# Decode step with cached attention and a bilinear GLU on one core: first five loads in three, last head's V weighed in two places

## The chip, the core and the metric

One core of a Trainium2 chip. The metric is the device time of one execution in microseconds (us), as the median over runs. The core has a matrix engine (TensorE, "PE" in the profile, its weight loads "PEld"), a vector engine (VectorE, "DVE"), a scalar engine (ScalarE, "ACT"), a general engine (GpSimd, "POOL"), and a sync engine (SyncE, "SP") that here issues all transfers. 16 DMA engines move data from the chip's memory (HBM) into the on-chip memory (SBUF), which has 128 partitions. TensorE writes its results into PSUM.

## The reference

One decode step for two sequences (B = 2): layernorm of x, attention of 32 heads over the last 2048 positions of a K and V cache, a bilinear GLU, and a residual. All in float32.

```python
B, Sq, D = 2, 1, 512
Hq, Hkv, Sk, Dh = 32, 32, 8192, 128          # F = 1376
W = min(4096, max(256, Sk // 4))             # 2048
xn = _layernorm(x)
q = (xn @ wq).reshape(B, Sq, Hq, Dh)...
scores = einsum("bhqd,bhkd->bhqk", q, k[:, :, Sk - W:]) * Dh ** -0.5
o = einsum("bhqk,bhkd->bhqd", softmax(scores), v[:, :, Sk - W:])
out = x + o.reshape(B, Sq, Hq * Dh) @ wo + ((xn @ w_gate) * (xn @ w_up)) @ w_down
```

The caches that are read make 2 x 2 x 32 x 2048 x 128 x 4 bytes = 134 MB; with the weights the core reads 159.5 MB, each byte once, for little arithmetic.

## The kernel before

**Layout of the data.** The host lays all inputs out as one long array, `stream`, in the order in which the kernel wants them. `blocks()` (L40) lists it: each block belongs to a tile (the key) and has fields, of which each is so many columns of 128 partitions. `("k", h)` is the K of head h for both sequences (4096 columns, 2 MB), `("v", h)` its V, `("wq", h)` a part of the query projection for a later group of heads, `("wo", h)` head h's rows of the output projection (512 columns), `("w", 0)` and `("w", 1)` the query projection of the first group (first head, other three), `("wg"/"wu", half)` halves of the gate and up projections, `("wd", i)` 128 rows of w_down. `wd(n)` takes the rows `WD[n]`. One block is one DMA.

**Buffers and queue.** There are three big SBUF tiles (`BUFS = 3`) of 13,824 columns. `pump()` (L137) issues on SP's queue the loads for which a tile is free; `done()` (L163) counts a field as used up, and with a tile's last field the tile is free and `pump()` goes on. So a load waits for the last reader of the tile three loads earlier. Only the first block, with key `q` (x, w part 0, three tables of ones called pick, rows and carry, and x once more as rows, `xr`, for the residual), has a small tile of its own, `first`. Loads 1 to 4 after it bring head 0's K with w part 1; the first half of gate and up with head 1's K; the second half with head 2's K; head 3's K, head 0's V and five blocks of w_down. Then follow 18 loads of three units each (a unit is the K of one head or the V of one, which runs `LAG = 3` heads behind K). The end: head 31's K with head 28's V; then into one tile head 29's V and head 30's V, one load each; into the last tile head 31's V in two halves (`v0`, and `v1` with wo), w_down's blocks 5 to 7, 8 and 9, and its last 96 rows, which come from a second array.

**Per head.** DVE multiplies K by the broadcast q in place (`products`, L265) and sums over 128 elements (`sums`, L273), 4.42 us each. `maxima` and `weights` (L278, L286) make the softmax numerators with DVE, POOL and ACT; `reciprocals` their sums. `weigh` (L317) multiplies V by them on TensorE, 4 matmuls per sequence and head into one of two PSUM tiles `o_ps`; `copy_out` (L326) brings these to SBUF on ACT and changes to the other tile; `transpose` (L333) is 4 small matmuls with `pick` and an ACT copy that scales by the reciprocals; `project_o` (L352) multiplies by wo. In the trace each TensorE operation in float32 shows as two matmuls.

**The output sum.** Up to head `HF - 1 = 25`, results add up in `acc`, 17 rows by 512. For the tail the sum changes its form: `accumulate` (L305) writes four matmuls of 128 columns, each to its own rows, so that the last addition and the output need only 128 columns. The old sum is carried over by a copy to SBUF (`acc_sb`, on DVE) and a matmul with `carry`. `down` (L409) adds the w_down blocks: part 0 to `acc`, the later ones by `accumulate`.

**Order.** Each engine runs its instructions in the order in which they are written (`InOrder`, L77). `keep_busy(n)` is a matmul of n columns whose result nobody reads. The tail, from L449, is written out by hand: head 30's and 31's K on DVE; on TensorE heads 26 and 27, then 28, 29, 30 and 31, each weighing, transposes, projection, with fillers between. At the end stand w_down's parts 1 and 2, head 31's projection, and the residual (`o_out`, L486), then the output's DMA.

Of the kernel before, what the change touches and what calls it, by code (L numbers as in the profile page):

```python
# [35 lines left out]
STEP = 3 * UNIT  # L36
WD = [(0, 5), (5, 8), (8, NFC)]


def blocks():  # L40

    def wd(n):
        return [("wd", i, D) for i in range(*WD[n])]

    def k(h):
        first = [("w", 1, CQ - NC * DH)] if h == 0 else []
        return [("k", h, CK)] + first + ([("wq", h, CP)] if h + HG < H else [])

    def v(h):
        return [("v", h, CK), ("wo", h, CO)]

    def gu(half):
        n = NC * (FH[half][1] - FH[half][0])
        return [("wg", half, n), ("wu", half, n)]  # L60

    units = []
    for h in range(LAG, H - 1):
        units += [k(h), v(h - LAG)]
    loads = [k(0), gu(0) + k(1), gu(1) + k(2), units[0] + units[1] + wd(0)]
    loads += [sum(units[i : i + 3], []) for i in range(2, len(units), 3)]
    loads += [k(H - 1) + v(H - 1 - LAG)]
    ones = [("pick", 0, 8 * B), ("rows", 0, NFB * B), ("carry", 0, M)]
    out = [(("q", 0), [("x", 0, B * NC), ("w", 0, NC * DH)] + ones + [("xr", 0, P)])]
    out += [(("s", i), fields) for i, fields in enumerate(loads)]  # L70
    late, last = ("s", len(loads)), ("s", len(loads) + 1)
    out += [(late, v(H - 3)), (late, v(H - 2)), (last, [("v0", H - 1, CK // 2)])]
    out += [(last, [("v1", H - 1, CK // 2), ("wo", H - 1, CO)])]
    return out + [(last, wd(n)) for n in range(1, len(WD))]

# [32 lines left out]
def kernel(  # L108
    ctx: ExitStack,
    tc: tile.TileContext,  # L110
    stream: bass.AP,
    wd_rest: bass.AP,
# [24 lines left out]
    def pump():  # L137
        nonlocal held
        while todo:
            key, fields, at = todo[0]  # L140
            if key not in tiles:
                if key[0] == "q":
                    n = sum(w for _, _, w in fields)
                    tiles[key] = const.tile([P, n], F32, name="first")
                elif held == BUFS:
                    return
                else:
                    held += 1
                    tiles[key] = steps.tile([P, STEP], F32, name="step")
# [12 lines left out]

    def done(kind, i):  # L163
        nonlocal held
        _, key = got.pop((kind, i))
        left[key] -= 1
        if left[key] == 0 and key[0] != "q":
# [6 lines left out]
    pick = got["pick", 0][0].rearrange("p (r s b) -> p r s b", s=2, b=B)  # L174
    rows, carry, x_nat = got["rows", 0][0], got["carry", 0][0][:M], got["xr", 0][0]

# [21 lines left out]
    for t in oT_ring:  # L198
# [10 lines left out]
        xc, xT, tr[:, 0:B].unsqueeze(2).to_broadcast([P, B, NC]), op=ALU.subtract  # L209
    )  # L210
    dve.tensor_tensor(sq, xc, xc, op=ALU.mult)
    dve.tensor_reduce(st[:, 1, :], sq, axis=AX.X, op=ALU.add)
# [10 lines left out]
        xnb, xn.rearrange("p c b -> p (c b)").unsqueeze(2).to_broadcast([P, NC * B, P])  # L223
    )

    q_ps, s_t, mm_t, p_t, sum_t, rec_t, o_sbs, oT = {}, {}, {}, {}, {}, {}, {}, {}
# [23 lines left out]
    def project_q(h):  # L250

        g, c = h // HG + 1, h % HG
        if c == 0:
# [98 lines left out]
    def project_o(h):  # L352
        wo = got["wo", h][0]
        if h < HF:
            pe.matmul(acc, oT.pop(h), wo, start=(h == 0), stop=(h == HF - 1))
        else:
            accumulate(oT.pop(h), wo)
        done("wo", h)
# [50 lines left out]
    def down(n):  # L409
        for c in range(*WD[n]):  # L410
            if n == 0:
                pe.matmul(acc, hT[:, c % 4, c // 4, :], got["wd", c][0], start=False, stop=False)
            else:
                accumulate(hT[:, c % 4, c // 4, :], got["wd", c][0])
            done("wd", c)


    HF = H - 6
    spare_in = xnb.rearrange("p a b -> p (a b)")
    project_first(0)  # L420
    for _, fields in blocks()[1:]:
        ks = [i for kind, i, _ in fields if kind == "k"]
        vs = [i for kind, i, _ in fields if kind == "v"]
        if not ks:
            break
        if vs and vs[-1] >= H - 5:
            break
        for n, h in enumerate(ks):
            products(h)
            if h == 0:  # L430
                project_first(1)
            if h + HG < H:
                project_q(h)
# [25 lines left out]
    keep_busy(GC)  # L459
    accumulate(carry, acc_sb)  # L460
    project_o(HF)
    project_o(HF + 1)
    keep_busy(GC)
# [3 lines left out]
    sums(h + 1)  # L467
    values([H - 4], ((GC, 256), (GC,)))
    weights(h)
# [22 lines left out]
def laid_out(x):  # L492

    import numpy as np

    a = x["A_x"].reshape(B, D)
    first = {
        kind: np.zeros((P, w), a.dtype) for kind, _, w in blocks()[0][1] if kind != "w"
    }
    first["x"][:] = a.reshape(B, P, NC).transpose(1, 0, 2).reshape(P, B * NC)  # L500
    for b in range(B):
# [5 lines left out]
        first["carry"][RB * b, RB * b] = 1.0  # L507
        first["xr"][RB * b :: 32, :] = a[b].reshape(D // P, P)
    cache = {
# [31 lines left out]
    ]  # L541
    return {"stream": np.concatenate(parts), "wd_rest": wd[NFC * P :]}

# [30 lines left out]
```

## Time and profile before

| | |
|---|---|
| median of 3 runs | 379.82 us (379.79 to 380.61) |
| the profiled execution: time | 380.0 us |
| its span, first to last instruction | 378.2 us |
| HBM read | 159.54 MB, 422 GB/s over the span |
| DVE busy | 294.2 us (78%) |
| PE busy | 258.9 us (68%) |
| ACT busy | 58.2 us (15%) |
| mean granted TensorE clock | 0.788 |

The page of the profile cuts the span in 40 slices, with a digit for the busy share of each engine in tenths. The chain of waits is followed back from the last instruction: at each step to what released it. In a timeline a line has the start, the time, engine, line of the kernel (nearly all have L92, the helper that keeps the order), operation, tiles out<-in, count, and the idle time before it with what ended it. A window's line has busy times and counts of PE, PEld, DVE, ACT and POOL, then the granted clock, the busy share of the DMA engines and their rate.

### The profile page before, as it was taken

To read this page: it belongs to the slowest core of one execution; us is meant where nothing else is said; L and a number is where in the kernel's file an instruction comes from. 1 tells how busy PE (TensorE), PEld (TensorE's weight loads), DVE (VectorE), ACT (ScalarE), POOL (GpSimd) and SP (SyncE) were. 2 spreads that over 40 slices of the span, in tenths; PEclk is the share of its full clock that TensorE was granted. 3 is DMA by queue.
4 is the path that set the end of the run, shared out by engine and by line. 5 is a ranking of instruction groups with operands and counts; after the bars stand their busy time and mean duration, and the time that the engine had idled before them with its cause. 6 is when DMAs were issued, how large, how long until landed. Compare 5 with 4: busy or idle time off the path is not lost.

```text
span 378.2 us, 2866 instructions
## 1 busy us (share of the span) xinstructions
PE 258.9 (68%) x1090; PEld 88.4 (23%) x1090; DVE 294.2 (78%) x144; ACT 58.2 (15%) x255; POOL 25.4 (7%) x78
## 2 busy tenths in 40 slices
PE   3929878848557487854838685485867638637986
PEld 3501222312122122211212221121212203022433
DVE  3739762999499499859949976994997799599950
ACT  1020012102020211202021120111102011111231
POOL 1000000001000000000000010000000000000000
PEclk9967968868596966859686688976669888556999
DMA  8999999999999999999999999999999999999993
GB/s 328 475 411 421 465 444 404 462 427 415 459 393 456 450 404 450 429 415 462 398 451 446 404 450 433 421 452 428 415 456 409 440 446 433 434 411 425 414 415 141
DMA packets 4456, 159.71 MB, mean 422 GB/s; under 512 B 500, under 2 KB 508, under 8 KB 988
## 3 DMA queue, kind: packets, MB, share of 16 engines
q1 hardware_dynamic: 4444, 159.54, 98.0%
q8 instruction: 8, 0.13, 0.1%
q14 instruction: 4, 0.03, 0.0%
HBM read 159.54 MB, written 0.00 MB: 422 GB/s over the span
## 4 chain that ended last, share of the span: by engine, by line
DMA 67%; PE 16%; DVE 14%; ACT 1%; issue 0%; SPq 0%; DVEq 0%
DMA step<-in_stream_dram 67%; PE o_ps L92 8%; DVE s L92 7%; DVE step L92 7%; PE q L92 5%; PE acc L92 2%; PE tr L92 1%; ACT o_sb L92 1%; ACT oT L92 0%; SPq L92 0%; DVE m L92 0%; DVE o_out L92 0%; DVE rec L92 0%; DVEq L92 0%
## 5 line engine op out<-in xcount | busy, mean ns | idle before, releaser
L92 DVE TENSOR_TENSOR step<-step,q 128x4096 f32<-128x4096 f32 x31 | 136.6, 4407 | 59.8 <-DMA step<-in_stream_dram 59.8
L92 PE MATMUL q<-step,xnb 128*128 128x512 f32 (+1 forms) x128 | 94.8, 888 | 75.5 <-DMA step<-in_stream_dram 75.5
L92 DVE TENSOR_REDUCE s<-step 128x32 f32<-128x4096 f32 x32 | 141.4, 4420 | 1.1
L92 PE MATMUL o_ps<-step,p 128*16 128x512 f32 x512 | 70.7, 688 | 10.4 <-DMA step<-in_stream_dram 10.4
L92 PEld LDWEIGHTS q<-step,xnb 128*128 128x128 f32 x128 | 32.4, 278 | 130.2 <-DMA step<-in_stream_dram 78.4
L92 PE MATMUL acc<-step,oT 128*17 128x512 f32 (+1 forms) x100 | 34.8, 518 | 9.8 <-ACT oT L92 9.8
L92 ACT COPY o_sb<-o_ps 128x512 f32<-128x512 f32 x24 | 14.0, 585 | 148.1 <-PE o_ps L92 148.1
L92 PE MATMUL tr<-first,o_sb 128*128 128x2 f32 (+2 forms) x192 | 26.2, 257 | 14.5 <-ACT o_sb L92 12.8
L92 PEld LDWEIGHTS tr<-first,o_sb 128*128 128x128 f32 x192 | 24.6, 197 | 34.9 <-ACT o_sb L92 32.2
L283 POOL PARTITION_ALL_REDUCE mm<-m x32 | 11.3, 354 | 299.3 <-DVE rec L92 191.0
L92 PEld LDWEIGHTS o_ps<-step,p 128*16 128x16 f32 x512 | 13.4, 107 | 73.9 <-issue 58.8
L92 ACT ACTIVATE nm<-mm 128x2 f32<-128x2 f32 x32 | 6.5, 203 | 129.4 <-POOL mm L283 129.4
L92 ACT ACTIVATE p<-s,nm 128x16 f32<-128x16 f32 x64 | 19.2, 300 | 1.0
L92 ACT ACTIVATE oT<-tr,rec 128x1 f32<-128x1 f32 x64 | 12.2, 260 | 28.3 <-PE tr L92 28.3
L299 POOL PARTITION_ALL_REDUCE sum<-rs x32 | 12.7, 398 | 41.0 <-ACT p L92 41.0
L92 PE MATMUL o_ps<-step,xn 128*2 128x512 f32 (+1 forms) x48 | 13.0, 597 | 0.0
L92 ACT ACTIVATION_READ_ACCUMULATOR p<-s,nm 128x1 f32 x64 | 12.0, 187 | 0.0
L92 PE MATMUL q<-xnb,mean_w 128*128 128x512 f32 (+1 forms) x24 | 11.6, 580 | 0.0
L92 PEld LDWEIGHTS acc<-step,oT 128*17 128x17 f32 x100 | 4.8, 98 | 18.6 <-ACT oT L92 12.5
L92 DVE TENSOR_TENSOR step<-step,tr 128x4096 f32<-128x4096 f32 x1 | 4.4, 4420 | 3.9 <-DMA step<-in_stream_dram 3.9
L92 PE MATMUL acc<-step,hT 128*17 128x128 f32 (+2 forms) x58 | 7.3, 350 | 0.0
L92 DVE TENSOR_TENSOR o_out<-acc,first 128x128 f32<-128x128 f32 x1 | 0.3, 290 | 8.9 <-PE acc L92 8.9
(34 smaller groups left out, 39.7 us busy)
## 6 DMA issues: line engine op xcount, KB each, us to landing
step<-in_stream_dram SPq DMA_DIRECT2D x16, 6912.0 KB, 31.1
step<-in_stream_dram SPq DMA_DIRECT2D x2, 6400.0 KB, 30.0
step<-in_stream_dram SPq DMA_DIRECT2D x1, 6656.0 KB, 29.2
step<-in_stream_dram SPq DMA_DIRECT2D x1, 5888.0 KB, 30.0
step<-in_stream_dram SPq DMA_DIRECT2D x2, 2304.0 KB, 16.0
step<-in_stream_dram SPq DMA_DIRECT2D x1, 4352.0 KB
step<-in_stream_dram SPq DMA_DIRECT2D x1, 3712.0 KB, 33.1
step<-in_stream_dram SPq DMA_DIRECT2D x1, 3072.0 KB, 10.1
```

What stands on the lines that cost most here:

```text
L92: made = call(*args, **kwargs)
L283: nc.gpsimd.partition_all_reduce(mm, m, P, bass_isa.ReduceOp.max)
L299: nc.gpsimd.partition_all_reduce(sum_t[h], rs, P, bass_isa.ReduceOp.add)
```

## The change

- **First loads.** The block `q` and its tile `first` are gone. x, the three tables, both parts of w and the K of heads 0 and 1 (with their wq parts) are one load of 11,311 columns into a big tile. The second load has the first half of gate and up with head 2's K (12,800 columns), the third the second half with head 3's K, head 0's V and three blocks of w_down (13,568). These three fill the three tiles. The tables are copied to a small tile `ones` by three DVE copies, as their big tile is to be freed.
- **Residual.** x as rows comes by a DMA of its own from a small array, 8 rows of 512 bytes, into a tile that DVE has set to zero. It stands fourth on SP's queue.
- **Start of the computation.** Both parts of the first projection run one after the other before head 0's products. The GLU halves go with heads 2 and 3 rather than 1 and 2, and `gate()` stands in head 3's turn ahead of head 0's values.
- **w_down.** Parts (0,3), (3,5), (5,8), (8,10): blocks 3 and 4 move from load 4 to the load of head 31's K. They are added to `acc` by `down(1)` after head 28's weighing. `HF` is 28 rather than 26, so heads 26 and 27 go to `acc` too, and the copy `acc_sb` is made later, on ACT.
- **Last loads.** Head 31's second half of V is a load of its own; its wo comes with w_down's blocks 5 to 7.
- **Tail.** Head 31's first half is weighed after head 30's weighing and one filler, ahead of head 30's transposes, where ACT copies head 30's result. Of the fillers there, one of 512 and the one of 512 between the two halves become two of 256.

```diff
-WD = [(0, 5), (5, 8), (8, NFC)]
+WD = [(0, 3), (3, 5), (5, 8), (8, NFC)]
...
-        first = [("w", 1, CQ - NC * DH)] if h == 0 else []
-        return [("k", h, CK)] + first + ([("wq", h, CP)] if h + HG < H else [])
+        return [("k", h, CK)] + ([("wq", h, CP)] if h + HG < H else [])
...
-    loads = [k(0), gu(0) + k(1), gu(1) + k(2), units[0] + units[1] + wd(0)]
+    ones = [("pick", 0, 8 * B), ("rows", 0, NFB * B), ("carry", 0, M)]
+    first = [("x", 0, B * NC)] + ones + [("w", 0, NC * DH), ("w", 1, CQ - NC * DH)]
+    loads = [first + k(0) + k(1), gu(0) + k(2), gu(1) + units[0] + units[1] + wd(0)]
     loads += [sum(units[i : i + 3], []) for i in range(2, len(units), 3)]
-    loads += [k(H - 1) + v(H - 1 - LAG)]
-    ones = [("pick", 0, 8 * B), ("rows", 0, NFB * B), ("carry", 0, M)]
-    out = [(("q", 0), [("x", 0, B * NC), ("w", 0, NC * DH)] + ones + [("xr", 0, P)])]
-    out += [(("s", i), fields) for i, fields in enumerate(loads)]
+    loads += [k(H - 1) + v(H - 1 - LAG) + wd(1)]
+    out = [(("s", i), fields) for i, fields in enumerate(loads)]
...
-    out += [(last, [("v1", H - 1, CK // 2), ("wo", H - 1, CO)])]
-    return out + [(last, wd(n)) for n in range(1, len(WD))]
+    out += [(last, [("v1", H - 1, CK // 2)]), (last, [("wo", H - 1, CO)] + wd(2))]
+    return out + [(last, wd(n)) for n in range(3, len(WD))]
...
+    x_nat = const.tile([P, P], F32, name="x_nat")
+    dve.memset(x_nat, 0.0)
+    sp.dma_start(x_nat[::RB, :], x_rows)
...
+    for kind in ("pick", "rows", "carry"):
+        t = got[kind, 0][0]
+        n += t.shape[1]
+        dve.tensor_copy(ones[:, n - t.shape[1] : n], t)
+        done(kind, 0)
...
-            if n == 0:
-                pe.matmul(acc, hT[:, c % 4, c // 4, :], got["wd", c][0], start=False, stop=False)
+            if n < 2:
+                pe.matmul(
+                    acc, hT[:, c % 4, c // 4, :], got["wd", c][0],
+                    start=False, stop=(c == WD[1][1] - 1),
+                )
...
-    HF = H - 6
+    HF = H - 4
...
-            if 1 <= h <= 2:
-                project_gu(h - 1)
+            if 2 <= h <= 3:
+                project_gu(h - 2)
             sums(h)
+            if h == LAG:
+                gate()
             if vs and n == 0:
                 values(vs)
             if h == LAG:
                 down(0)
-            if h == 2:
-                gate()
...
-    acc_sb = const.tile([M, D], F32, name="acc_sb")
-    dve.tensor_copy(acc_sb, acc)
     products(h)
     sums(h)
-    o_sb = pv([HF, HF + 1])
-    keep_busy(GC)
-    keep_busy(256)
-    transpose([HF, HF + 1], o_sb)
-    keep_busy(GC)
-    accumulate(carry, acc_sb)
-    project_o(HF)
-    project_o(HF + 1)
+    values([H - 6, H - 5], ((GC, 256), (GC,)))
     keep_busy(GC)
...
-    values([H - 4], ((GC, 256), (GC,)))
+    o_sb = pv([HF])
+    down(1)
+    acc_sb = const.tile([M, D], F32, name="acc_sb")
+    act.copy(acc_sb, acc)
+    transpose([HF], o_sb)
+    keep_busy(256)
+    accumulate(carry, acc_sb)
+    project_o(HF)
...
-    values([H - 2], ((GC,), ()))
+    o_sb = pv([H - 2])
+    keep_busy(256)
     weigh(H - 1, 0, got["v0", H - 1][0], True, False)
-    keep_busy(GC)
+    transpose([H - 2], o_sb)
+    keep_busy(256)
+    project_o(H - 2)
     weigh(H - 1, 1, got["v1", H - 1][0], False, True)
     o_sb = copy_out()
     keep_busy(256)
     transpose([H - 1], o_sb)
-    down(1)
+    down(2)
     project_o(H - 1)
-    down(2)
+    down(3)
```

More of the change, by code (lines that the diff above doesn't have):

```diff
@@ L110 @@
     tc: tile.TileContext,
+    x_rows: bass.AP,
     stream: bass.AP,
@@ L141, in pump @@
             if key not in tiles:
[L142 to L145, printed above, removed]
+                if held == BUFS:
                     return
-                else:
-                    held += 1
-                    tiles[key] = steps.tile([P, STEP], F32, name="step")
+                held += 1
+                tiles[key] = steps.tile([P, STEP], F32, name="step")
                 used[key] = 0
@@ L166, in done @@
         left[key] -= 1
-        if left[key] == 0 and key[0] != "q":
+        if left[key] == 0:
             del tiles[key]
@@ L173 @@
     xT = got["x", 0][0].rearrange("p (b c) -> p b c", b=B)
-    pick = got["pick", 0][0].rearrange("p (r s b) -> p r s b", s=2, b=B)
-    rows, carry, x_nat = got["rows", 0][0], got["carry", 0][0][:M], got["xr", 0][0]
+    x_nat = const.tile([P, P], F32, name="x_nat")
+    dve.memset(x_nat, 0.0)
+    sp.dma_start(x_nat[::RB, :], x_rows)
     mean_w = const.tile([P, P], F32, name="mean_w")
@@ L210 @@
     )
+    done("x", 0)
     dve.tensor_tensor(sq, xc, xc, op=ALU.mult)
@@ L224 @@
     )
+    ones = const.tile([P, sum(w for _, _, w in blocks()[0][1][1:4])], F32, name="ones")
+    n = 0
+    for kind in ("pick", "rows", "carry"):
[3 more added lines that the diff above has]
+        done(kind, 0)
+    pick = ones[:, : 8 * B].rearrange("p (r s b) -> p r s b", s=2, b=B)
+    rows, carry = ones[:, 8 * B : 8 * B + NFB * B], ones[:M, 8 * B + NFB * B :]
     q_ps, s_t, mm_t, p_t, sum_t, rec_t, o_sbs, oT = {}, {}, {}, {}, {}, {}, {}, {}
@@ L250, in project_q @@
     def project_q(h):
+        if h + HG >= H:
+            return
         g, c = h // HG + 1, h % HG
@@ L354, in project_o @@
         if h < HF:
-            pe.matmul(acc, oT.pop(h), wo, start=(h == 0), stop=(h == HF - 1))
+            pe.matmul(acc, oT.pop(h), wo, start=(h == 0), stop=False)
         else:
@@ L415, in down @@
             done("wd", c)
-    HF = H - 6
+    HF = H - 4
     spare_in = xnb.rearrange("p a b -> p (a b)")
-    project_first(0)
-    for _, fields in blocks()[1:]:
+    for i in range(2):
+        project_first(i)
+    for _, fields in blocks():
         ks = [i for kind, i, _ in fields if kind == "k"]
         vs = [i for kind, i, _ in fields if kind == "v"]
-        if not ks:
-            break
         if vs and vs[-1] >= H - 5:
@@ L429 @@
             products(h)
[L430 to L433, printed above, removed]
[L434 to L435 removed]
+            project_q(h)
+            if 2 <= h <= 3:
+                project_gu(h - 2)
             sums(h)
+            if h == LAG:
+                gate()
             if vs and n == 0:
@@ L497, in laid_out @@
     first = {
-        kind: np.zeros((P, w), a.dtype) for kind, _, w in blocks()[0][1] if kind != "w"
+        kind: np.zeros((P, w), a.dtype) for kind, _, w in blocks()[0][1][:4]
     }
@@ L507, in laid_out @@
         first["carry"][RB * b, RB * b] = 1.0
-        first["xr"][RB * b :: 32, :] = a[b].reshape(D // P, P)
     cache = {
@@ L541, in laid_out @@
     ]
-    return {"stream": np.concatenate(parts), "wd_rest": wd[NFC * P :]}
+    return {
+        "x_rows": a.reshape(B, D // P, P).transpose(1, 0, 2).reshape(-1, P),
+        "stream": np.concatenate(parts), "wd_rest": wd[NFC * P :],
+    }
 _INS = ["A_x", "A_k_cache", "A_v_cache", "A_wq", "A_wo", "B_w_gate", "B_w_up", "B_w_down"]
```

## The prediction

> **What bounds the kernel now.** First the head of the page and its chain of waits.
>
> ```profile
> span 378.2 us, 2866 instructions
> DMA  8999999999999999999999999999999999999993
> DMA 67%; PE 16%; DVE 14%; ACT 1%; issue 0%; SPq 0%; DVEq 0%
> ```
>
> The DMA engines are busy in every slice but the first and the last, and two thirds of the chain is waiting for a landing. Busy shares of the other engines (DVE 78%, PE 68%) hide that. Next, the windows, to see where the stream begins and ends (columns: window, length, busy time and count of PE, PEld, DVE, ACT, POOL, granted clock, DMA share, GB/s).
>
> ```profile
> 1.00:2.00 1.00, 0.00 (x0) 0.00 (x0) 0.85 (x2) 1.00 (x1) 0.81 (x9) 1.00 0.42 55
> 2.00:3.00 1.00, 0.00 (x0) 0.00 (x0) 0.60 (x2) 0.00 (x1) 0.00 (x0) 1.00 0.96 327
> 3.00:4.00 1.00, 0.03 (x1) 0.03 (x1) 0.16 (x1) 0.00 (x0) 0.00 (x0) 1.00 0.99 364
> 1.70:371.50 369.80, 255.22 (x1024) 85.70 (x1024) 293.15 (x140) 56.21 (x252) 24.19 (x67) 0.78 1.00 431
> 371.50:373.20 1.70, 1.62 (x12) 0.93 (x8) 0.00 (x0) 0.58 (x1) 0.00 (x0) 1.00 0.51 189
> ```
>
> From 1.7 to 371.5 us the share is 1.00 at 431 GB/s: there is no hole in the stream, so a shorter compute stage in the middle is worth nothing. Only three things can move the end: the bytes, the slow first microseconds, and what is left to do after the last loads land. For that last part, the issues of the final loads with their time to landing, and the TensorE timeline of the tail.
>
> ```profile
> step<-in_stream_dram SPq DMA_DIRECT2D x1, 1280.0 KB, 14.5
> step<-in_stream_dram SPq DMA_DIRECT2D x1, 1024.0 KB, 11.8
> step<-in_stream_dram SPq DMA_DIRECT2D x1, 768.0 KB, 16.1
> step<-in_stream_dram SPq DMA_DIRECT2D x1, 512.0 KB, 16.9
> step<-in_wd_rest_dram SPq DMA_DIRECT2D x1, 192.0 KB, 16.9
> ```
>
> ```profile
> 364.30 1.91 PE L92 MATMUL o_ps<-step,p 128*16 128x512 f32 x16 [0.44 <-DMA step<-in_stream_dram]
> 366.13 1.13 PE L92 MATMUL q<-xnb,mean_w 128*128 128x512 f32 x2
> 367.10 0.95 PE L92 MATMUL tr<-first,o_sb 128*128 128x2 f32 x8
> 368.55 0.41 PE L92 MATMUL acc<-step,oT 128*17 128x128 f32 x8 [0.50 <-ACT oT L92]
> 368.78 1.04 PE L92 MATMUL o_ps<-step,p 128*16 128x512 f32 x8
> 369.75 1.13 PE L92 MATMUL q<-xnb,mean_w 128*128 128x512 f32 x2
> 370.81 1.05 PE L92 MATMUL o_ps<-step,p 128*16 128x512 f32 x8
> 371.79 0.70 PE L92 MATMUL q<-xnb,mean_w 128*128 128x256 f32 x2
> 372.56 1.05 PE L92 MATMUL tr<-first,o_sb 128*128 128x2 f32 x8
> 373.55 0.85 PE L92 MATMUL acc<-step,hT 128*17 128x128 f32 x24
> ```
>
> SP's timeline has those loads issued at 355.32, 354.94, 355.79, 356.26 and 356.73 us (in the order of the rows), so they land at 369.8 (second half of head 31's V), 366.7 (first half), 371.9, 373.2 and 373.6. Head 30's V landed at 364.25 (the chain's DMA piece ends there). From then TensorE is the bound: it has no idle time but 0.50 us, and o_out starts at 375.34, 1.7 us after the last landing. The `q<-xnb,mean_w` rows are fillers that compute nothing.
>
> **The change, part by part.** The sum is made against the profiled execution: span 378.2, time 380.0, so 1.8 us lies around the span. The median of the runs is 379.82; I take the difference off that.
>
> *Tail (−1.3).* After v30's matmuls the order becomes: filler of 256, first half of head 31, transposes of head 30, filler of 256, projection of head 30, second half of head 31, then as before. In start-to-start times of the rows above: head 30's weighing 1.83 (366.13−364.30); filler of 256, half of the 512's 1.06 (370.81−369.75), 0.53; half a head 0.97 (369.75−368.78); transposes and the way to the projection 1.45 (368.55−367.10), of which the second filler covers the ACT wait, so 0.96+0.53 = 1.49; projection 0.23; from the second half to o_out 4.53 (375.34−370.81). Sum 9.58, against 11.04 (375.34−364.30) now: −1.46. Two landings answer back. The first half, landing 2.5 us after v30, is wanted 2.36 us after: +0.1. The second half now lands alone, 256 KB less at 431 GB/s, so at 369.2, before it is wanted at 369.45. wo with three w_down blocks ends at the byte where w_down's first part ended (371.9) and is wanted at 372.2. The last landing, 373.63, stays where it is, and behind it stand the last 8 matmuls, about 0.4 (24 of them plus the drain took 375.34−374.33 = 1.01): o_out not before 374.08. So the tail gives 375.34−374.08 = 1.26.
>
> *Head 28's stage (0, covered).* down(1), two 512-wide projections (2×0.43 by half of the warm half-head row), and the ACT copy of acc (0.66 by the DVE row it replaces) now lie between v28 (353.4) and v29 (358.8). Work there: 1.84 weighing, 0.87, transposes 0.96, filler 0.53, carry and projection 0.23 each, 4.7 us in a gap of 5.4. Without that cover it would delay v29's and v30's weighing, which itself has 0.44 us of idle before it. DVE loses the 0.66 us copy; its 31st head ends earlier, and its weights were not late.
>
> *Bytes (−0.15).* The 64 KB of x rows shrink to 4 KB: 0.06 MB at 431 GB/s. w_down's two parts move from load 4 to the load of the last K, so everything in between lands 0.52 MB (1.2 us) earlier and from there on nothing moves.
>
> *Start (−0.25).* Up to 4.0 us the windows moved 55+327+364 KB·1000 = 0.75 MB, where 2.3 us at 431 give 0.99: a loss of 0.55 us. How much of it belongs to the 2.7 KB rows of the first load and how much to a cold start, which stays, no row tells: between 0 and −0.55; I take −0.25, about half, since the share is already 0.96 while the rate is low. [...]
>
> *What the big first load delays (0, covered).* x, both w parts and the K of heads 0 and 1 are one load of 128×11311×4 = 5.79 MB. Now 3.49 MB have landed at 11.3 (DVE resumes at 11.35); 2.30 MB more at 431 GB/s make 16.6. From landing to first products took 11.35−3.75 = 7.6 us less a wait of 0.25: 7.35 (layernorm 3.6, first projection 3.75). Then two heads on DVE, 4×4.42+0.3 = 17.9: the first buffer is free at 41.9, the fourth load's bytes flow about 1 us after. The three loads queued at the start hold 19.3 MB, 44.8 us, so the stream runs until 46.5. Cover: 3.6 us. The next releases have 10 us (second load's K done at about 51, stream fed to 62.8) and some 7 (gate, which now stands ahead of head 0's values: third buffer free near 72, stream fed to 79). x's own little DMA is issued behind the three loads, waits for a memset over by 1.1, and stands before nothing due until 41.9.
>
> Sum: −1.26−0.15−0.25 = −1.66: span 376.5, profiled 378.3, and **378.2** by the median.
>
> **Rivals.**
>
> *The last bytes bind more than I say (20%).* The stream's end takes the place of TensorE. For it: o_out is already set by a landing in my sum. Against: the same bytes are left after v30. With no gain at the start, and the last landing up to 0.5 late through the new boundaries, o_out starts at 374.0 to 374.6: 378.5 to 379.1.
>
> *Head 28 comes late (8%).* If the clock warms one step later and the ACT copy waits, pv(29) and pv(30) slip; 0.7 and 0.4 us of slack are used first. For it: 4.7 us in 5.4. It eats the tail's 1.26 if 2.2 us late: 379.5, no change.
>
> *The queue runs dry (6%), slower.* The place is the wait for the fourth load; it decides once the first buffer is free later than 45.5. For it: LayerNorm, both projections and two heads now stand in series behind one landing. Against: 3.6 us of cover. Should one more projection (3.75) and matmuls at half the clock stand before the products, 6 to 7 us in all: a hole of 2.4 to 3.4, net +0.7 to +1.7: 381.0.
>
> *The tail runs at half clock (4%), slower.* The granted clock fell to 0.58 in 22 to 23 us, after TensorE had idled from 18.73. At 0.5 the same 16 matmuls took 3.62 instead of 1.91; the 6.0 us of the new sum up to the second half of head 31 that are TensorE rows would double: +6.0−1.66: 384.2. Against: no idle time over about 1 us is left between 353 and the end, by the order above. [...]
>
> **How the numbers follow.** Forecast 62%, rivals 20, 8, 6 and 4. A measurement here tells 0.2% (0.76 us) from no change, so faster means below 379.06: nearly all of the forecast and most of the first rival, 0.74. Within: the rest of that rival, the second, a little of the third, 0.16. Slower: 0.10. Range: 377.6 (start −0.55, and 0.2 of scatter) to 379.4 (second rival all but reached).
>
> **What would show it.** Right: head 31's first half-head directly after one filler behind v30's weighing; o_out starting 0.4 to 0.5 us after the last landing; DMA share 1.00 from 1.7 to 371; the fourth load issued near 42. Wrong: a window with DMA share below 0.9 at 44 to 50 us; TensorE idle before v30's weighing gone; a granted clock of 0.5 after 350; a last landing not earlier than 373.6.

## The result, and the profile after

| | before | after |
|---|---|---|
| median, runs on the same chip | 379.88 us (379.69 to 380.61, 14 runs) | 379.19 us (379.06 to 379.63, 14 runs) |
| profiled execution: time, span | 380.0, 378.2 us | 379.26, 377.5 us |
| o_out starts | 375.34 us | 374.59 us |

The ratio is 0.998, with a 95% interval of 0.9972 to 0.9989. The kernel became faster by 0.69 us. The forecast was 1.66 on the profiled execution (1.62 on the median), so the sign held, and less than half of the size came.

The page of the kernel after: span, share of the DMA engines in 40 slices, chain by engine.

```profile
span 377.5 us, 2835 instructions
DMA  9999999999999999999999999999999999999994
DMA 54%; DVE 23%; PE 18%; issue 2%; ACT 2%; SPq 0%; DVEq 0%
```

The stream still fills every slice, now the first one too. The windows of the kernel after, with the columns as before:

```profile
1.00:2.00 1.00, 0.00 (x0) 0.00 (x0) 0.84 (x4) 1.00 (x1) 0.81 (x9) 1.00 1.86 543
2.00:3.00 1.00, 0.00 (x0) 0.00 (x0) 0.75 (x2) 0.00 (x0) 0.00 (x0) 1.00 0.52 181
3.00:4.00 1.00, 0.00 (x0) 0.00 (x0) 0.00 (x0) 0.00 (x0) 0.00 (x0) 1.00 0.00 0
1.70:371.50 369.80, 250.24 (x1010) 85.56 (x1010) 292.76 (x143) 57.06 (x254) 24.29 (x67) 0.80 1.00 431
371.50:373.20 1.70, 1.65 (x33) 1.64 (x37) 0.00 (x0) 0.41 (x2) 0.00 (x0) 1.00 0.51 163
```

From 1.7 to 371.5 us the share is 1.00 at 431 GB/s, as before. The first three lines look like a burst and a hole, and are neither: a row of the new first load is 45 KB long and 13 of the 16 first ones take 2.17 to 2.86 us, and a row is counted whole in the window in which it starts (12 rows start in the first window, 12 x 45.2 = 543 KB). With rows that long, single windows of a microsecond can't be read. Together the three moved (543 + 181 + 0) KB·1000 = 0.72 MB, against 0.75 MB before: here already nothing is seen of a faster start.

The tail of the kernel after, TensorE first and then the last addition on DVE:

```profile
364.45 1.91 PE L90 MATMUL o_ps<-step,p 128*16 128x512 f32 x16 [0.28 <-DMA step<-in_stream_dram]
366.29 0.70 PE L90 MATMUL q<-xnb,mean_w 128*128 128x256 f32 x2
367.03 1.05 PE L90 MATMUL o_ps<-step,p 128*16 128x512 f32 x8
368.01 1.05 PE L90 MATMUL tr<-ones,o_sb 128*128 128x2 f32 x8
368.93 0.68 PE L90 MATMUL q<-xnb,mean_w 128*128 128x256 f32 x2
369.57 0.41 PE L90 MATMUL acc<-step,oT 128*17 128x128 f32 x8
369.80 1.04 PE L90 MATMUL o_ps<-step,p 128*16 128x512 f32 x8
370.77 0.70 PE L90 MATMUL q<-xnb,mean_w 128*128 128x256 f32 x2
371.55 1.05 PE L90 MATMUL tr<-ones,o_sb 128*128 128x2 f32 x8
372.53 0.85 PE L90 MATMUL acc<-step,hT 128*17 128x128 f32 x24
373.20 0.40 PE L90 MATMUL acc<-step,oT 128*17 128x128 f32 x8
373.61 0.85 PE L90 MATMUL acc<-step,hT 128*17 128x128 f32 x24
374.59 0.29 DVE L90 TENSOR_TENSOR o_out<-acc,x_nat 128x128 f32<-128x128 f32 x1 [9.70 <-PE acc L90]
```

Head 31's first half stands one filler behind head 30's weighing, and the idle 0.50 us in front of a projection is gone. From head 30's weighing to o_out it is 374.59 − 364.45 = 10.14 us, where it was 11.04. The line to look at is the last of TensorE: it starts 0.41 us after the projection ahead of it. In the kernel before these two stood 0.22 apart:

```profile
374.21 0.40 PE L92 MATMUL acc<-step,oT 128*17 128x128 f32 x8
374.43 0.84 PE L92 MATMUL acc<-step,hT 128*17 128x128 f32 x24
375.34 0.29 DVE L92 TENSOR_TENSOR o_out<-acc,first 128x128 f32<-128x128 f32 x1 [8.94 <-PE acc L92]
```

In the kernel after, the weight loads of this last group have the wait in their line:

```profile
373.60 0.57 PEld L90 LDWEIGHTS acc<-step,hT 128*17 128x17 f32 x24 [0.29 <-DMA step<-in_stream_dram]
```

The trace records 16 landings of a load, as many as it has data rows under way at a time; they are read here as one of each DMA engine. What waits for the load starts only behind the last of them (head 30's V before: the mean of its landings at 363.31, the last at 364.25, its weighing at 364.30). So a mean engine and the slowest can be told apart (us from the span's start):

```
                        mean engine    slowest engine
                       before   after   before   after
V of head 30           363.31  363.27   364.25  364.41
V of 31, first half    365.79  365.75   366.74  366.90
V of 31, second half   368.89  368.24   369.82  369.38
w_down blocks 8, 9     372.31  372.28   373.16  373.56
last 96 rows           372.85  372.95   373.63  373.94
```

Apart from the second half, which the change lets land alone and so earlier, and the last rows (0.10 late), the mean engine is 0.03 to 0.04 early. The slowest is 0.16 late at head 30's V and 0.40 late at w_down's blocks 8 and 9, on which the last 24 matmuls wait: 373.56, they start at 373.61, and 0.98 later o_out starts.

### The profile page after: what moved, and what is told of

Read it like the earlier page. It is cut to its first block, busy times and chain, and to the rows that moved or that the text cites. A ratio compares the mean times of both kernels' runs of the same rounds, so it can differ in the third digit from the quotient of the medians.

```text
span 377.5 us, 2835 instructions
## 1 busy us (share of the span) xinstructions
PE 253.1 (67%) x1074; PEld 87.9 (23%) x1074; DVE 293.8 (78%) x147; ACT 58.5 (15%) x256; POOL 25.5 (7%) x78
## 4 chain that ended last, share of the span: by engine, by line
DMA 54%; DVE 23%; PE 18%; issue 2%; ACT 2%; SPq 0%; DVEq 0%
DMA step<-in_stream_dram 54%; DVE step L90 12%; DVE s L90 11%; PE o_ps L90 6%; PE acc L90 4%; PE tr L90 4%; PE q L90 4%; ACT o_sb L90 1%; ACT oT L90 0%; DVE m L90 0%; DVE o_sb L90 0%; ACT hT L90 0%; SPq L90 0%; DVE rec L90 0%; DVE st L90 0%
## 5 line engine op out<-in xcount | busy, mean ns | idle before, releaser
L90 PE MATMUL q<-step,xnb 128*128 128x512 f32 (+1 forms) x128 | 88.5, 839 | 64.7 <-DMA step<-in_stream_dram 64.7
L90 PEld LDWEIGHTS q<-step,xnb 128*128 128x128 f32 x128 | 31.2, 265 | 117.0 <-DMA step<-in_stream_dram 66.7
L90 PE MATMUL acc<-step,oT 128*17 128x512 f32 (+1 forms) x88 | 36.2, 567 | 9.3 <-ACT oT L90 8.1
L90 PE MATMUL tr<-ones,o_sb 128*128 128x2 f32 (+2 forms) x192 | 28.0, 266 | 17.6 <-ACT o_sb L90 12.8
L90 PEld LDWEIGHTS tr<-ones,o_sb 128*128 128x128 f32 x192 | 26.0, 207 | 39.9 <-ACT o_sb L90 32.4
L90 PE MATMUL tr<-st,mean_w 128*128 128x2 f32 x4 | 1.2, 363 | 17.8 <-DVE st L90 17.8
L90 PE MATMUL o_ps<-step,xn 128*2 128x512 f32 (+1 forms) x48 | 12.1, 552 | 0.0
L90 PE MATMUL q<-xnb,mean_w 128*128 128x512 f32 (+1 forms) x20 | 8.8, 528 | 0.0
L90 PE MATMUL acc<-step,hT 128*17 128x128 f32 (+2 forms) x58 | 8.2, 364 | 0.0
```

Of the source, the lines that this page charges most:

```text
L90: made = call(*args, **kwargs)
```

## The experiments

Every run stands against runs of the kernel before on the same chip in the same series; a ratio has its 95% interval. e1 to e4 are one series, e5 to e8 a second, e9 and e10 a third, each on another chip.

| run | median (range) | before | ratio | o_out, profiled |
|---|---|---|---|---|
| e1: before, new tail only | 378.93 (378.73–379.05) | 380.13 | 0.9962 [0.9949, 0.9975] | 374.23 |
| e2: after, old tail | 380.30 (379.94–381.23) | 380.13 | 1.0002 [0.9992, 1.0013] | 375.51 |
| e3: after, small first load | 379.63 (379.23–380.00) | 380.13 | 0.9981 [0.9973, 0.9990] | 375.14 |
| e4: after, `gate()` earlier | 379.16 (379.01–379.35) | 380.13 | 0.9968 [0.9957, 0.9980] | 374.52 |
| e5: after, once more | 379.38 (379.06–380.50) | 380.14 | 0.9978 [0.9965, 0.9992] | 375.18 |
| e6: e1 and x rows apart | 378.87 (378.76–379.26) | 380.14 | 0.9969 [0.9957, 0.9981] | 373.97 |
| e7: e1, later projection | 378.68 (378.65–379.26) | 380.14 | 0.9966 [0.9953, 0.9978] | 373.88 |
| e8: e1, no fillers at the end | 380.01 (379.02–382.79) | 380.14 | 1.0003 [0.9983, 1.0022] | 374.35 |
| e9: after, old first loads | 379.00 (378.68–379.14) | 379.98 | 0.9972 [0.9961, 0.9982] | 374.13 |
| e10: e7 and x rows apart | 378.83 (378.74–379.72) | 379.98 | 0.9970 [0.9960, 0.9980] | 374.58 |

### e1: the kernel before, with the new tail alone

```diff
-    out += [(last, [("v1", H - 1, CK // 2), ("wo", H - 1, CO)])]
-    return out + [(last, wd(n)) for n in range(1, len(WD))]
+    out += [(last, [("v1", H - 1, CK // 2)]), (last, [("wo", H - 1, CO)] + wd(1))]
+    return out + [(last, wd(n)) for n in range(2, len(WD))]
...
-    values([H - 2], ((GC,), ()))
+    o_sb = pv([H - 2])
+    keep_busy(256)
     weigh(H - 1, 0, got["v0", H - 1][0], True, False)
-    keep_busy(GC)
+    transpose([H - 2], o_sb)
+    keep_busy(256)
+    project_o(H - 2)
     weigh(H - 1, 1, got["v1", H - 1][0], False, True)
```

> The kernel before, with nothing of the change but the tail: head 31's first half weighed in the wait for head 30's copy, its second half of V loaded alone, wo with w_down's blocks 5 to 7. Theory A (the stream's end is late for a reason at the start or in the middle, and the tail is worth what its own steps say): the last landings stay at 373.2 (w_down 8, 9) and 373.6, behind the first of these stand 24 matmuls and the drain, 1.0 us, so o_out starts at 374.2 instead of 375.3: -1.1, median 378.8. Theory B (the new tail itself delays the last landings, by its loads of other sizes): w_down's 8, 9 land about 0.4 later and the gain is -0.7, median 379.2, as the whole change.

The median fell by 380.13 − 378.93 = 1.20 us, and the slowest of its runs (379.05) is below the fastest run of the whole change (379.06, in another series). So the tail alone seems to bring more than the change as a whole; e5 and e6 have both in one series. The end of e1 on TensorE and DVE:

```profile
364.36 1.91 PE L92 MATMUL o_ps<-step,p 128*16 128x512 f32 x16 [0.45 <-DMA step<-in_stream_dram]
...
373.10 0.40 PE L92 MATMUL acc<-step,oT 128*17 128x128 f32 x8
373.32 0.84 PE L92 MATMUL acc<-step,hT 128*17 128x128 f32 x24
374.23 0.29 DVE L92 TENSOR_TENSOR o_out<-acc,first 128x128 f32<-128x128 f32 x1 [7.76 <-PE acc L92]
```

From head 30's weighing it is 374.23 − 364.36 = 9.87 us, a gain of 1.17. Blocks 8 and 9 landed at 373.22 here, and the last group follows the projection at the old distance of 0.22. This is Theory A.

### e2: the whole change, with the tail of before

The diff of e1 the other way, on the kernel after.

> The changed kernel with the tail's loads and order from head 30 on as before; so it has only the first loads in three, x as rows by itself, w_down's moved parts and the copy of acc on ACT. By the prediction (bytes -0.15, start -0.25) head 30's V lands 0.4 earlier and the median is 379.5. Theory A: the start gives nothing and the slowest DMA engine is later than before, head 30's V lands at 364.2 to 364.4, median 379.8 to 380.1. Theory B: no delay without the new tail, 379.5 to 379.7.

No change was measured: the interval reaches from 0.3 us faster to 0.5 slower, and the 0.40 forecast for start and bytes lies outside. Head 30's weighing and o_out in e2:

```profile
364.40 1.91 PE L90 MATMUL o_ps<-step,p 128*16 128x512 f32 x16 [0.31 <-DMA step<-in_stream_dram]
375.51 0.29 DVE L90 TENSOR_TENSOR o_out<-acc,x_nat 128x128 f32<-128x128 f32 x1 [10.71 <-PE acc L90]
```

That is 0.10 later than in the kernel before (364.30) at the weighing, and 11.11 us from there instead of 11.04. With e1, this divides the result: all the gain is the tail's, and the rest of the change (first loads, x rows, w_down's moved blocks, the copy on ACT) brings nothing by itself.

### e3: a small load ahead of the merged one

```diff
-    first = [("x", 0, B * NC)] + ones + [("w", 0, NC * DH), ("w", 1, CQ - NC * DH)]
+    first = [("w", 0, NC * DH), ("w", 1, CQ - NC * DH)]
...
-    out = [(("s", i), fields) for i, fields in enumerate(loads)]
+    out = [(("q", 0), [("x", 0, B * NC)] + ones)]
+    out += [(("s", i), fields) for i, fields in enumerate(loads)]
```

x and the tables come ahead in a tile of their own, so that layernorm runs while the rest loads.

> The changed kernel, but x and the three tables are a load of their own again (47 columns, 24 KB) into a small tile, ahead of the first big load, and the three table copies go. The theory that the cold start falls unequally on the 16 engines when their first rows are of 45 KB, and that the landings, which wait for the slowest engine, stay later for that to the end: the 16 engines' ends of the first big load lie within 0.3 of their mean instead of 0.53, the last landings come 0.2 to 0.3 earlier, median 378.9 to 379.0. Rival (the cold start costs the same whatever comes first, and the skew comes from elsewhere): 379.2, and the mean over the engines unchanged.

The theory that asked for it fell: the slowest engine ended the big load 0.60 us behind the mean, not within 0.3. The rival fell too, as the mean moved: the big load landed at 16.74 on the mean engine, where it landed at 16.34 without the small one, so the small load cost 0.4 us of stream, which was still there at head 30's V (363.64 against 363.27). The gain over the kernel before is 0.50 us, 0.2 to 0.3 less than the 0.69 and 0.76 of the whole change in two other series; the intervals overlap. Starting layernorm early buys nothing, since nothing at the end waits for it.

### e4: the third buffer free earlier

```diff
-            sums(h)
             if h == LAG:
                 gate()
+            sums(h)
```

> The changed kernel with the gate one step earlier, ahead of head 3's sums, so that the third buffer is free about 4.4 us sooner: the sixth load is issued near 72.6 instead of 77.0, where the stream reaches it at 79.5. Theory (a load issued only 2.5 us ahead of its turn starts with slow rows, 0.4 and 0.5 on two engines in the trace): no slow rows at 79.5, the landing of that load and the next 0.1 to 0.5 earlier, median 379.0 to 379.2. Rival (those rows are slow for another reason): they stay, median 379.2.

The prediction had the third buffer free near 72 us. These are SP's issue of the sixth load in the kernel after, and then in e4:

```profile
77.03 0.33 SPq L90 DMA_DIRECT2D step<-in_stream_dram  x1
```

```profile
72.08 0.33 SPq L90 DMA_DIRECT2D step<-in_stream_dram  x1
```

TensorE in the kernel after, up to that issue, shows why it was late:

```profile
60.91 0.59 PE L90 MATMUL tr<-ones,o_sb 128*128 128x6 f32 x2 [4.01 <-DVE o_sb L90]
...
63.98 3.61 PE L90 MATMUL o_ps<-step,p 128*16 128x512 f32 x16
68.29 1.87 PE L90 MATMUL tr<-ones,o_sb 128*128 128x2 f32 x8 [0.71 <-ACT o_sb L90]
70.75 1.87 PE L90 MATMUL acc<-step,oT 128*17 128x512 f32 x2 [0.59 <-ACT nm L90]
72.41 4.59 PE L90 MATMUL acc<-step,hT 128*17 128x512 f32 x6
```

The gate's transposes waited 4.01 us for its DVE work, which stood behind head 3's `sums` (55.84 to 60.17 on DVE); behind it the weighing took 3.61 us at a granted clock of 0.50, where the tail's takes 1.91 at 1.00, and the w_down matmuls ran 4.59 us, up to 77.0. The first DMA engine was through with the fifth load at 79.5, so the sixth was issued only 2.5 us ahead of its turn. In e4 the wait is 0.86, and the load is issued 7.4 us ahead; the weighing takes 3.58 there too, so the long wait isn't what made the clock slow. Of the theory's two parts one held. Two engines took 2.44 and 2.57 us for their first row of the sixth load in the kernel after, where 2.04 is usual; in e4 no engine took over 2.05. But the load landed no earlier on the mean engine: 96.77, against 96.70. The median is 0.97 below before, against 0.69 and 0.76 for the kernel after in two other series, and the runs lie closer together (0.34 us). The intervals overlap, so a gain of 0.2 may be there and isn't shown.

### e5: the kernel after once more

> The changed kernel once more, on the chip of the other runs of this group. Theory A (the new tail is worth 1.2 and the rest of the change costs 0.3 to 0.5, in every execution): 0.6 to 0.8 under the kernel before. Rival (the missing part was the scatter of one group of executions, in which DMA engine was late): 1.0 to 1.2 under it.

The gain was 0.76 us this time. Its interval reaches from 0.3 to 1.3 us, so alone it doesn't tell the theories apart. But in the same series five of the six runs of e6, which has the new tail and the x rows, took at most 379.03 us, and none of the eleven here took less than 379.06: the rest of the change does give something back. The profiled execution took 379.85 us, more than the median of 379.38, and the trace shows where it lost: the sixth load, issued at 77.32, needed 97.15 − 80.24 = 16.91 us on the mean engine from the landing of the fifth, where the first profile of the same kernel has 96.70 − 80.32 = 16.38, e4 16.44 and e9 16.34. Nearly all engines took 2.3 to 2.9 us for their first row of it or their second, instead of 2.04. The half microsecond lost there stayed lost: head 30's V landed at 363.70 on the mean engine. The traces order by how early the load was issued: 2.2 us ahead of its turn nearly all engines have a slow row (e5), at 2.5 two of 16 (the kernel after), at 3.1 one (e2, issued at 76.39), at 7 and more none (e3, e4, e9). That is one execution each, so it is a hint at the cause and no proof.

### e6: new tail, and x rows as a load of their own

```diff
-    out = [(("q", 0), [("x", 0, B * NC), ("w", 0, NC * DH)] + ones + [("xr", 0, P)])]
+    out = [(("q", 0), [("x", 0, B * NC), ("w", 0, NC * DH)] + ones)]
...
+    x_nat = const.tile([P, P], F32, name="x_nat")
+    dve.memset(x_nat, 0.0)
+    sp.dma_start(x_nat[::RB, :], x_rows)
```

The tail is e1's.

> The kernel before with the new tail alone, and x as rows by a small transfer of its own as in the change, so that the first load is 64 KB shorter; no other part of the change. By the bytes, 0.06 MB at 431 GB/s, the whole stream comes 0.15 earlier: 1.3 to 1.4 under the kernel before. Rival (what the bytes give is taken back: the first load's slow rows cost what they cost by their number, and the end's small rows, from an array that now lies elsewhere, take 0.10 instead of 0.09 each): 1.1 to 1.2 under it, as the new tail alone, and the mean landing of head 30's V unchanged at 363.25.

The gain is 1.27 us, against 1.20 in e1 and in another series. The 64 KB less would be 0.15 us by the rate. Head 30's V landed at 363.11 on the mean engine, 0.14 ahead of e1, as Theory A has it; but in e7, with x rows in the first load, it landed at 363.13. Whether the 64 KB are worth 0.07 or nothing is taken up in e10.

### e7: head 30's projection behind head 31's second half

```diff
-WD = [(0, 5), (5, 8), (8, NFC)]
+WD = [(0, 5), (5, 8), (8, 9), (9, NFC)]
...
     transpose([H - 2], o_sb)
-    keep_busy(256)
-    project_o(H - 2)
     weigh(H - 1, 1, got["v1", H - 1][0], False, True)
     o_sb = copy_out()
+    project_o(H - 2)
     keep_busy(256)
     transpose([H - 1], o_sb)
     down(1)
     project_o(H - 1)
     down(2)
+    down(3)
```

> The kernel before with the new tail, and in it head 30's projection behind head 31's second half (in the wait for head 31's copy, one filler less), and w_down's blocks 8 and 9 in two loads. By the steps of the tail the second half starts 0.35 earlier, with its landing near 369.3; the end is then set by the landings: behind block 9's, near 373.2, stand 16 matmuls and the drain, 0.8 instead of 1.0, so o_out at 374.0 to 374.1: 0.2 less than the new tail alone, 1.3 to 1.4 under the kernel before. Rival (one more small load costs the stream what it spares): as the new tail alone, 1.2 under.

This has the lowest median: 380.14 − 378.68 = 1.46 us, though its interval overlaps those of e1, e6 and e10. Its tail:

```profile
368.98 1.05 PE L92 MATMUL o_ps<-step,p 128*16 128x512 f32 x8 [0.24 <-DMA step<-in_stream_dram]
369.85 0.40 PE L92 MATMUL acc<-step,oT 128*17 128x128 f32 x8
...
372.61 1.21 PE L92 MATMUL acc<-step,hT 128*17 128x128 f32 x24
373.88 0.29 DVE L92 TENSOR_TENSOR o_out<-acc,first 128x128 f32<-128x128 f32 x1 [7.75 <-PE acc L92]
```

Now the second half waits for its landing, and the last 24 matmuls are stretched to 1.21 us, since they take each block as it lands. The last rows landed at 373.36 and o_out started 0.52 later. This is the state that the prediction had expected of the change itself: an end set by the last landing, not by TensorE. The chain of waits of e7 says the same.

```profile
356.93 16.43 DMA step<-in_wd_rest_dram
373.40 0.46 PE acc L92 x8
373.88 0.29 DVE o_out L92
```

### e8: new tail without fillers from head 28 on

The diff takes out the `keep_busy` calls from head 28's values to the end.

> The kernel before with the new tail and without the fillers from head 28's weighing on. Theory that the fillers are needed: TensorE then idles 1 to 3 us before each landing, the granted clock falls to 0.5 and the tail's weighings take 3.6 instead of 1.9: 2 or more slower than the new tail with them. Rival (the idle times left are too short for that): the clock stays 1.00 from 353 to the end, same time within 0.2, as the waits they fill end with landings.

The profiled execution, at 379.02 us, was as fast as e1, with idle times of 0.5 to 0.9 us in front of most groups. But even in it the granted clock fell. These are the weighing of head 30 with the first half of head 31, and the windows around it (the granted clock is the third number from the end):

```profile
364.07 4.04 PE L92 MATMUL o_ps<-step,p 128*16 128x512 f32 x24 [0.92 <-DMA step<-in_stream_dram]
```

```profile
363.00:364.00 1.00, 0.15 (x8) 0.00 (x0) 0.97 (x3) 0.00 (x0) 0.00 (x0) 0.63 0.89 369
364.00:365.00 1.00, 0.93 (x8) 0.25 (x12) 0.01 (x1) 0.47 (x3) 0.36 (x1) 0.50 0.96 401
365.00:366.00 1.00, 1.00 (x12) 0.24 (x8) 0.00 (x0) 0.42 (x4) 0.40 (x1) 0.50 1.01 418
366.00:367.00 1.00, 1.00 (x8) 0.14 (x4) 0.17 (x1) 0.00 (x0) 0.00 (x0) 0.66 1.06 442
```

The clock was at 0.50 from 363.26 to 366.67 us, so the rival's "stays 1.00 from 353 to the end" is wrong, and the theory's idle times of 1 to 3 us weren't needed: none since 353 was longer than 0.92. It cost this execution little, as the slow matmuls took the time in which the fillers stand: the first half of head 31 was weighed by 368.1, against 368.0 in e1, and o_out came at 374.35 instead of 374.23. The other runs did worse. The 11 spread from 379.02 to 382.79, with a median of 380.01, 1.1 us above e1 and e6: without the fillers nearly the whole gain of the tail is gone, though not the 2 or more that the theory had. The two slowest had a mean granted clock of 0.774 and 0.769, where the others of e8 had 0.778 to 0.797 and e1's six runs 0.787 to 0.801. Only the one execution was profiled, so where the others lost their time isn't seen.

### e9: everything but the merged first loads

The first loads of the kernel before, the rest as in the kernel after (x rows apart, w_down's blocks 3 and 4 with the last K, head 28 behind the change of form, the new tail).

> The changed kernel with the first loads of the kernel before (x, the tables and w part 0 in a small load ahead, K of heads 0, 1 and 2 in a load each), and with everything else of the change: x rows as a load of their own, w_down's blocks 3 and 4 with the last K, head 28 after the sum's change of form, the new tail. It asks which part of the change gives back some 0.5 us of what the new tail alone brings (1.2 us). Theory A: the merged first loads do it (late sixth load, slower first rows); then this kernel is 1.2 us faster than before, near 378.9, as the new tail alone is. Theory B: moving w_down's blocks to the end does it (the stretch from head 30's V to the last bytes takes 0.13 us longer on the mean engine in all kernels that have it); then this kernel stays 0.7 us faster, near 379.4, and the stretch takes 9.68 us here too, not 9.55.

The gain is 0.98 us, between the 1.2 of Theory A and the 0.7 of Theory B, and its interval (0.7 to 1.5) holds both. The stretch from head 30's V to the last landing took 372.65 − 363.14 = 9.51 us on the mean engine and not 9.68, so the reason that Theory B gives falls. The load whose issue was late in the kernel after, with its turn near 80, was issued at 60.90, and blocks 8 and 9 landed at 372.88 on the slowest engine, 0.75 behind the mean.

### e10: e7, and x rows as a load of their own

The diffs of e6 and e7 together.

> Head 30's projection behind head 31's second half and w_down's blocks 8 and 9 in two loads (378.68 before this run, 1.46 us below the kernel before), and x rows as a load of their own. Theory A (bytes count wherever they lie): 0.15 us below the kernel without the small load, so 1.6 us faster than before. Theory B (the 64 KB lie in the first load, whose rows are slow whatever their size): no gain from them, 1.4 to 1.5 us faster than before.

The gain is 1.15 us, less than e7's 1.46 in another series, with intervals that overlap; no gain from the 64 KB is seen. The landing of the second load (head 0's K) is where it would have to show first. On the mean engine it landed at 10.97, 10.92, 10.76 and 10.88 us with x rows in the first load (before, e1, e7, e8), and at 10.76, 10.77 and 10.77 without (e6, e9, e10). So they are worth 0 to 0.15 us, and one execution scatters by more. Bad luck shows in e10's profile: its slowest engine was 1.45 us behind the mean at block 9, and o_out followed at 374.58.

## Why the prediction had the tail right, the start wrong and the size too large

**The stream binds the middle: right.** The share stayed at 1.00, and DVE's busy time didn't matter.

**Where the size was lost.** The forecast had head 30's weighing 0.40 us earlier, at 363.90, and o_out 11.04 − 1.26 = 9.78 after it, at 373.68. Measured are 364.45 and 10.14, so o_out is 0.91 us late: 0.55 up to head 30's weighing, where start and bytes were to bring 0.40, and 0.36 behind it, in the tail. That is the first rival, given 20%, nearly as it was written: no gain at the start, the last landings up to 0.5 late, o_out at 374.0 to 374.6. One of the prediction's own signs of being wrong came with it, a last landing (373.94) not earlier than 373.6.

**The tail, −1.26: the step was right, its floor was not.** With nearly the landings of before, e1 has −1.17 in the steps and −1.20 in the median. In the kernel after it was −0.90. The step that failed is "The last landing, 373.63, stays where it is, and behind it stand the last 8 matmuls, about 0.4". The last landing came 0.31 later, and the landing that set the end was the one before it: 24 matmuls and the drain, 0.98 us, stand behind blocks 8 and 9. Even with their landing of before that makes 373.16 + 0.05 + 0.98 = 374.19, 0.11 past the forecast; they landed 0.40 later, which makes 374.59, the measured start of o_out. A smaller miss is the filler of 256: it took 0.62 us (366.08 to 366.70 in e7), not half of 1.06, and there are two of them, so e1's steps make 9.87 us where the prediction's make 9.58 and a wait of 0.1. That wait, of the first half for its landing, was some 0.1, as forecast.

**Start −0.25 and bytes −0.15: wrong; measured 0 with an interval of −0.3 to +0.5.** This is the failed step that weighs most. The prediction laid the loss of the first microseconds about half to the 2.7 KB rows. The DMA rows of the trace show a loss on the first rows in both kernels. Before, the eight 2.7 KB rows of each engine took 1.27 us in the mean, 0.40 longer than eight rows at the later pace of 0.108, and the next rows 0.22, 0.62 in all; in the kernel after, the first 45 KB rows took 1.7 to 2.9 us, where later ones took 1.67, a mean loss of 0.70. With the old tail (e2), neither this nor the 64 KB moved the end.

**The third buffer "free near 72": mis-sized, it was 77.0.** The prediction gives no sum for its 72. In the trace the gate's wait for DVE (4.01 us) is in the way, and e4, which has 0.86 of it, issued the load at 72.08. The cover of "some 7" us was 2.5, and 2.2 in e5. It cost next to nothing on the mean engine in the first profile; in the other that load lost 0.5 us. The queue didn't run dry, but it came nearest to it at the sixth load and not at the fourth.

**The first buffer free at 41.9: right.** It was free at 42.2, where DVE ended head 1's `sums`; the first load had landed at 16.87 (forecast 16.6). DVE in the kernel after:

```profile
16.89 0.16 DVE L90 TENSOR_REDUCE st<-step 128x2 f32<-128x8 f32 x1 [14.09 <-DMA step<-in_stream_dram]
24.25 4.42 DVE L90 TENSOR_TENSOR step<-step,tr 128x4096 f32<-128x4096 f32 x1 [3.45 <-PE tr L90]
```

From the landing to the products are 7.36 us, forecast 7.35.

**Head 28's stage covered: right, but just.** TensorE in the kernel after between the V of heads 28 and 29:

```profile
353.49 1.91 PE L90 MATMUL o_ps<-step,p 128*16 128x512 f32 x16
355.22 1.88 PE L90 MATMUL acc<-step,hT 128*17 128x512 f32 x4
...
358.89 0.41 PE L90 MATMUL acc<-step,oT 128*17 128x128 f32 x8
359.12 0.61 PE L90 MATMUL o_ps<-step,p 128*16 128x512 f32 x4
```

`down(1)` took 1.88 us and not 0.87: its two products show as four matmuls of 0.47, and the forecast had counted two. Head 29's V had landed at 358.91 and was weighed from 359.12, so 0.2 us were overdrawn here. Head 30's weighing still had 0.28 us of idle time before it, so it cost the end nothing.

**The tail at half clock: did not come.** The granted clock was 1.00 in the last windows. But the ground given against it, that no idle time over about 1 us is left, isn't enough by itself: in e8 the clock was at 0.50 for 3.41 us behind idle times of at most 0.92 us; in e1, with the fillers, it stayed at 1.00.

**What stays open.** From e1's 1.20 to the 0.69 and 0.76 of the whole change, the medians of e9 would lay some 0.2 to 0.3 to the merged first loads, and e4's would have an earlier sixth load bring about as much back. All these steps are smaller than the intervals, so none of them is shown. In the profiled executions the loss sits in the slowest engine: at blocks 8 and 9 it was 1.14 to 1.39 us behind the mean in the five kernels with merged first loads (after, e2 to e5), and 0.72 to 0.96 in before, e1 and e6 to e9, but 1.45 in e10. The traces say in part why: the distance grows almost only in loads during which one engine has an instruction load (the last section). In the kernel after it went from 0.52 to 1.31 us over the first of these, from 1.25 to 1.69 over the second and from 1.14 to 1.36 over the last, while the five between brought it down by 0.1 each; in e10 it went from 1.00 to 1.33 over the seventh. So it seems to count whether an instruction load falls on an engine that is already behind; why it does in one execution and not in another is open.

## What to carry to other kernels

When the stream of loads binds, gain is to be had behind its last bytes: order the tail so that each load is used when it lands, and count the work behind the last landing but one too. A merged load saved nothing here, as its first rows lost 0.70 us where those of before lost 0.62, and it freed its buffer later (at 42.2 us, where the first big buffer of before was free at 20.3); check when each buffer comes free at the clock and with the waits of that stage. The sixth load had slow rows here where it was issued 2.2 to 3.1 us ahead of its turn, and none where it was issued 7 us ahead or more. Keep the fillers of a tail until runs, and not one profile, say that they can go. Test the parts of a change one by one: here one part was worth 1.2 us, and the rest nothing or a little less.

## What the runs showed of the hardware

**Instruction loads delay single DMA engines.** The page of the kernel after lists a second kind of traffic (packets, MB, share):

```profile
q8 instruction: 8, 0.13, 0.1%
```

Eight loads of 16 KB, one each near 53, 101, 151, 202, 251, 301, 348 and 371 us, each 1.02 to 1.11 us long; in the middle of the first six, 15 engines have a data row under way and not 16, so one engine brings no data meanwhile, and the row that follows takes 2.5 to 2.6 us instead of 2.04. Over the first of them the slowest engine goes from 0.52 to 1.31 us behind the mean (0.26 to 1.33 in the kernel before, whose first is at 41.3). From there on the loads landed 0.99 to 1.71 us behind the mean engine (0.78 to 1.47 before), in the loads ahead of it 0.52 to 0.53 (0.26 to 0.28), so 0.1% of the traffic goes with landings 0.5 to 1.2 us later. The last one falls in the last loads: at 370.1 to 371.1 in the kernel after and e1 to e10, at 368.0 in the kernel before.

**The first rows were slow at both lengths.** Some 0.6 to 0.7 us are lost at the start (0.62 with 2.7 KB rows before, 0.70 with 45 KB rows after), and a small load ahead added 0.4 (e3).

**The clock fell with gaps under 1 us.** In e8's profiled execution TensorE was busy for 2.11 and 2.09 us of the two stretches of 3.41 us ahead of 363.26, with no gap over 0.92, and then had a clock of 0.50 for 3.41 us; in e1, with fillers, it was busy for all of the same two stretches and kept 1.00. In every other profiled execution the clock was 1.00 from 348.1 us to past the last matmul.
